# The first x, its halo and the weights of a fused convolution and maxout kernel, loaded and prepared in another way

## The chip, the cores and the metric

The kernel runs on one core of a Trainium2 chip. The metric is the time on the device in microseconds (us); lower is better. Every time below comes from the profiled execution or from the timed runs of this kernel.

## What is computed

Two steps follow one another. The first is a causal convolution of width 7 along the sequence whose weights are made for each position and head by a softmax. The second is a maxout layer: two products with a hidden width of 1024, their elementwise maximum, and a product back to 192.

```python
# x: (8, 4160, 192), weight_gen: (8, 4160, 8 heads, 7 taps)
w = softmax(weight_gen, axis=-1)
x_pad = concatenate([zeros((B, 6, D)), x], axis=1)
y[b, s, h, g] = sum_k w[b, s, h, k] * x_pad[b, s + k, h, g]     # 24 channels a head
# moe_w1, moe_w2: (192, 1024), moe_w_out: (1024, 192)
out = maximum(y @ w1, y @ w2) @ w_out                           # (33280, 192) fp32
```

The kernel uses max(a, b) = a + relu(b - a): `wd` holds w2 - w1, `w10` holds w1 @ w_out, and out = relu(y @ wd) @ w_out + y @ w10.

## The kernel before

**Tiling.** The 33280 positions are cut into 128 partitions of 260 consecutive positions, so 16 partitions make one sequence. Each partition's 260 positions are worked on in 16 batches of 16 positions and a last one of 4. A partition needs the six positions ahead of its first one as well, the halo. For 112 of the 128 partitions the halo is the end of the partition before; for every sixteenth partition, where a sequence begins, it must be zero. `msk` holds 0 or 1 for each partition, and the halo of the first batch is multiplied by it. Later batches copy their halo from the batch before (the second DMA in `load_x`).

**Stages of a batch.** `exp_sum`, `red`, `ln`, `shift` and `weights` make the normalised tap weights `en_t` (ScalarE and VectorE in turn). `mul` is the VectorE product of x and the weights for all seven taps (L177). For the first batches the taps are summed and transposed by TensorE (`sum_transpose`, L243) and copied to `yt` by ScalarE (L250); later, VectorE adds the taps and a DMA transposes. `hid_tile` (L279) computes y @ wd on TensorE, `relu` (L289) evicts it on ScalarE, and `out_first`/`out_second` (L331 with `w10`, L319 with `wo`) make the output in PSUM. `evac` copies it out.

**Order.** The schedule is written out by hand: each engine runs its instructions in the order of the program text, and SyncE and GpSimd issue DMAs in that order too. SyncE's go into a hardware queue, GpSimd's into a software queue. From the fourth group of tiles on, a loop over groups of tiles issues the rest.

**The beginning, where the change lies.** SyncE issues `weight_gen` of batch 0 (L105), the halo of partitions 16 to 127 (L500), the first four positions of x (L507), four loads with the first 512 columns of w1 and w2 (L518; E is rows 0 to 127 and T rows 128 to 191, so `ws0E`, `ws1E`, `ws0T`, `ws1T`), positions 4 to 7, the other 512 columns, and `weight_gen` of batch 1. GpSimd issues the halo of partitions 1 to 15, and makes a partition index (L529) and the identity. All this x arrives as fp32 in `xs`. GpSimd (L540) and ScalarE (L542) multiply one half of the halo each by the mask into the bf16 tile `xb_t`. VectorE casts positions 0 to 3 (L546), and ScalarE positions 4 to 7 (L553). The first `mul` (L177) follows. `keep_warm` runs products of the identity on TensorE (L598) until then. VectorE subtracts w1 from w2 for half of the columns (L557, L561), ScalarE copies pieces of the result to the other partitions (L559, L560, L563); for the second half VectorE does both.

GpSimd waits for the last weight load of the first half with a one-element copy (`gate`, L566) and then issues further x loads, which cast to bf16 on the way, and `wo`. It also casts `w1T` (L573). `w1` in bf16 is transposed (L586), evicted (L648) and multiplied with `wo` on TensorE (L630), and five ScalarE copies (L642) put the result into `w10`.

Of the kernel before, what the change touches and what calls it, by code (L numbers as in the profile page):

```python
# [9 lines left out]
FP32 = mybir.dt.float32  # L10
BF16 = mybir.dt.bfloat16
I32 = mybir.dt.int32
AF = mybir.ActivationFunctionType
ALU = mybir.AluOpType
# [9 lines left out]
def kernel(  # L24
# [85 lines left out]

    def load_x(b, o, n, amid=lambda: None):

        if b not in xb_ts:
            xb_ts[b] = pxb.tile([P, (16 + PAD) * D], BF16, name="xb_t", tag="xb")
        nc.gpsimd.dma_start(  # L115
            out=xb_ts[b][:, (PAD + o) * D:(PAD + o + n) * D],
            in_=bass.AP(tensor=x.tensor, offset=(BATCHES[b][0] + o) * D,
                        ap=[[CPP * D, P], [1, n * D]]),
        )
        amid()  # L120
        if b > 0 and o == 0:
            nc.gpsimd.dma_start(out=xb_ts[b][:, 0:PAD * D],
                                in_=xb_ts[b - 1][:, 16 * D:(16 + PAD) * D])
# [367 lines left out]
    with tc.tile_pool(name="pstage", bufs=1) as pstage:  # L491
        ident_f = pstage.tile([P, P], FP32, name="ident_f")
        xs = pstage.tile([P, (PAD + 8) * D], FP32, name="xs")
        ws = {(kind, wi): pstage.tile([nr, F], FP32, name=f"ws{wi}{kind}")
              for kind, nr in (("E", P), ("T", 64)) for wi in range(2)}

        load_wg(0, nc.sync)
        nc.vector.memset(xs[0:1, 0:PAD * D], 0.0)
        for p0, p1, eng in ((16, P, nc.sync), (1, 16, nc.gpsimd)):
            eng.dma_start(  # L500
                out=xs[p0:p1, 0:PAD * D],
                in_=bass.AP(tensor=x.tensor, offset=(p0 * CPP - PAD) * D,
                            ap=[[CPP * D, p1 - p0], [1, PAD * D]]),
            )

        def load_first(o):
            nc.sync.dma_start(  # L507
                out=xs[:, (PAD + o) * D:(PAD + o + 4) * D],
                in_=bass.AP(tensor=x.tensor, offset=o * D, ap=[[CPP * D, P], [1, 4 * D]]),
            )  # L510

        load_first(0)
        HF = F // 2

# [8 lines left out]

        load_w(0)
        load_first(4)
        load_w(1)
        load_wg(1, nc.sync)

        nc.gpsimd.iota(msk_i, pattern=[[0, 1]], base=0, channel_multiplier=1)  # L529
        make_identity(nc, ident_f)  # L530
        nc.vector.tensor_single_scalar(out=msk_i, in_=msk_i, scalar=RPB - 1, op=ALU.bitwise_and)
        nc.vector.tensor_single_scalar(out=msk_i, in_=msk_i, scalar=1, op=ALU.min)
        nc.vector.tensor_copy(out=msk, in_=msk_i)
        nc.vector.tensor_copy(out=ident, in_=ident_f)  # L534
        for step in (exp_sum, red, ln, shift):
            for i in range(2):
                step(0, i, 2)
        xb_ts[0] = pxb.tile([P, (16 + PAD) * D], BF16, name="xb_t", tag="xb")
        HP = PAD * D // 2
        nc.gpsimd.tensor_scalar(out=xb_ts[0][:, 0:HP], in0=xs[:, 0:HP], scalar1=msk[:, 0:1], scalar2=None,  # L540
                                op0=ALU.mult)
        nc.scalar.activation(out=xb_ts[0][:, HP:2 * HP], in_=xs[:, HP:2 * HP], func=AF.Copy,  # L542
                             scale=msk[:, 0:1])
        for o in (0, 4, 8, 12):
            weights(0, o)
        nc.vector.tensor_copy(out=xb_ts[0][:, PAD * D:(PAD + 4) * D],  # L546
                              in_=xs[:, PAD * D:(PAD + 4) * D])
        mul(0, 0)
# [3 lines left out]
        nc.scalar.copy(out=w1["E"][:, 0:HF], in_=ws["E", 0][:, 0:HF])  # L552
        nc.scalar.copy(out=xb_ts[0][:, (PAD + 4) * D:(PAD + 8) * D], in_=xs[:, (PAD + 4) * D:])  # L553
        def w_diff(h, copy):
# [17 lines left out]
        )  # L572
        load_x(1, 0, 8, lambda: nc.gpsimd.tensor_copy(out=w1["T"], in_=ws["T", 0]))  # L573
        load_wg(2, nc.gpsimd)
# [25 lines left out]

        keep_warm(27)
        w_diff(0, nc.scalar.copy)
# [4 lines left out]

        nc.scalar.copy(out=w1["E"][:, HF:F], in_=ws["E", 0][:, HF:F])
        rd = room(0)
# [15 lines left out]
        def w10_product():  # L625

            pw = ps["o"].tile([P, 1024], FP32, name="pw", tag="op")
            for at, c0, nr in ((0, 0, P), (512, P, 64)):
                for fi in range(FCH):
                    nc.tensor.matmul(  # L630
                        pw[0:nr, at:at + D], lhsT=w1t[:, fi * D + c0:fi * D + c0 + nr],
                        rhs=wo[:, fi * D:(fi + 1) * D],
                        start=(fi == 0), stop=(fi == FCH - 1), skip_group_check=True,
                    )
            return pw

        def w10_copies(pw):

            for k, to, frm, at in ((0, 0, 0, 0), (1, 0, 64, 0), (2, 64, 0, 0), (1, 64, 0, 512),
                                   (2, 0, 0, 512)):  # L640
                nr = P if k == 0 else 64
                nc.scalar.copy(out=w10[to:to + nr, k * D:(k + 1) * D],  # L642
                               in_=pw[frm:frm + nr, at:at + D])

# [149 lines left out]
```

## Time and profile before

| | |
|---|---|
| median of 5 runs | 412.73 us (412.67 to 413.33) |
| profiled execution, own time | 412.73 us |
| its span, as the trace counts it | 410.9 us |
| TensorE busy | 397.8 us, 97% |
| VectorE busy | 376.7 us, 92% |
| ScalarE busy | 358.1 us, 87% |
| GpSimd busy | 81.6 us, 20% |
| granted TensorE clock | 1.00 |

Times in the profile run from the start of the span. A timeline row gives the start, the duration, the engine, the line in the program, the operation with its output and inputs, the shape and the count; in brackets stands how long the engine was idle before it and who ended that wait. Engine names: PE is TensorE, PEld its weight load, DVE VectorE, ACT ScalarE, POOL GpSimd, SP SyncE; a q behind a name means the engine's queue. The profiled execution took as long as the median, and about 1.8 us of it lie outside the span.

### The profile page before, as it was taken

How to read it: one execution, taken by the hardware profiler on the slowest of the kernel's cores; microseconds unless marked ns; L12 is line 12 of the kernel's file. 1: busy time of each engine (PE TensorE's matmuls, PEld its weight loads, DVE VectorE, ACT ScalarE, POOL GpSimd, SP SyncE). 2: the span in 40 equal slices, each digit the busy share in tenths (PEclk: the TensorE clock that was granted, in tenths of full speed). 3: DMA queues.
4: the chain of work that ended last, by engine and by line, in shares of the span. 5: the costliest groups of instructions: out<-in, count | busy, mean ns of one | idle time of the engine just before them, and what ended most of it. 6: DMA issues, size and time to landing. Idle time of an engine off the chain costs nothing.

```text
span 410.9 us, 15917 instructions
## 1 busy us (share of the span) xinstructions
PE 397.8 (97%) x7309; PEld 316.1 (77%) x7309; DVE 376.7 (92%) x219; ACT 358.1 (87%) x426; POOL 81.6 (20%) x104
## 2 busy tenths in 40 slices
PE   7898899999999999999999999999999999999995
PEld 2588899677777777777877778777777777787795
DVE  5999999999999999999999999999999999999100
ACT  6898998989989998899998999998989989888771
POOL 3720101222211212212012222210212222110000
PEclk9999999999999999999999999999999999999999
DMA  8975535765656965784785586478649637643613
GB/s 243 258 179 164 127 92 137 179 153 141 172 120 146 214 171 124 217 171 112 154 240 148 112 238 171 98 214 205 137 95 257 170 53 246 156 90 88 205 58 139
DMA packets 60242, 65.68 MB, mean 160 GB/s; under 512 B 47601, under 2 KB 48497, under 8 KB 60176
## 3 DMA queue, kind: packets, MB, share of 16 engines
q1 hardware_dynamic: 51904, 40.47, 34.1%
q0 software_dynamic: 8128, 24.11, 28.8%
q8 instruction: 57, 0.93, 0.9%
q10 hardware_dynamic: 144, 0.10, 0.1%
q14 instruction: 9, 0.07, 0.1%
HBM read 35.96 MB, written 25.56 MB: 150 GB/s over the span
## 4 chain that ended last, share of the span: by engine, by line
PE 83%; ACT 10%; issue 3%; DMA 2%; DVE 1%; SPq 1%; DVEq 0%; ACTq 0%
PE op_ps L319 38%; PE hd L279 36%; PE op_ps L331 7%; ACT rd_t L289 6%; DMA ws1T<-in_moe_w_dram 2%; ACT en_t L162 1%; PE hdp L279 1%; ACT o_t L375 1%; DVE wd L557 1%; ACT yt L250 0%; ACT e_t L130 0%; SPq L518 0%; ACT w1t L648 0%; DVE wd L561 0%; ACT w L642 0%
## 5 line engine op out<-in xcount | busy, mean ns | idle before, releaser
L289 ACT ACTIVATE rd_t<-hd 128x1024 bf16<-128x1024 f32 (+1 forms) x206 | 234.6, 1189 | 27.5 <-PE hd L279 26.1
L319 PE MATMUL op_ps<-wo,rd_t 64*128 64x192 bf16 x4160 | 210.5, 243 | 0.1
L319 PEld LDWEIGHTS <-rd_t 64*128 64x128 bf16 x4160 | 180.8, 94 | 15.7 <-ACTq L352 0.3
L279 PE MATMUL hd<-yt,wd 64*128 64x512 bf16 (+1 forms) x1584 | 187.3, 360 | 1.1 <-ACT rd_t L289 1.1
L177 DVE TENSOR_TENSOR m_t<-xb_t,en_t 128x10752 bf16<-128x10752 bf16 (+1 forms) x37 | 187.5, 5069 | 0.6 <-POOL xb_t L540 0.6
L279 PEld LDWEIGHTS <-wd 64*128 64x128 bf16 x1776 | 93.9, 94 | 44.8 <-issue 3.8
L219 POOL CAST gate<-yt 128x1 f32<-128x1 bf16 x29 | 41.3, 1425 | 272.4 <-DMA yt<-y_t 272.4
L193 DVE TENSOR_TENSOR m_t<-m_t 128x4608 bf16<-128x4608 bf16 (+1 forms) x33 | 78.1, 2368 | 0.1
L375 ACT COPY o_t<-op_ps 128x384 f32<-128x384 f32 (+1 forms) x99 | 57.2, 590 | 13.2 <-PE op_ps L319 12.9
L331 PE MATMUL op_ps<-w,yt 64*128 64x192 bf16 x780 | 55.5, 243 | 1.8 <-ACT o_t L375 1.4
L331 PEld LDWEIGHTS <-yt 64*128 64x128 bf16 x780 | 38.4, 94 | 18.5 <-issue 3.2
L199 DVE TENSOR_TENSOR m_t<-m_t 128x3072 bf16<-128x3072 bf16 (+1 forms) x29 | 49.9, 1722 | 0.1
L162 ACT ACTIVATE en_t<-wg_t 128x896 bf16<-128x896 f32 (+2 forms) x45 | 35.2, 816 | 0.3 <-DVE m_t L177 0.3
L202 DVE TENSOR_TENSOR y_t<-m_t 128x1536 bf16<-128x1536 bf16 (+1 forms) x29 | 27.3, 940 | 0.5
L365 DVE COPY o_t<-op_ps 128x192 f32<-128x192 f32 x1 | 0.4, 358 | 25.2 <-ACT o_t L365 25.2
L151 DVE TENSOR_TENSOR wg_t<-wg_t,sum_t 128x280 f32<-128x280 f32 (+5 forms) x46 | 22.0, 480 | 0.0
L115 POOL DMA_DIRECT2D xb_t<-in_x_dram x32 | 17.3, 540 | 22.6 <-DVE m_t L177 22.0
L142 DVE TENSOR_REDUCE sum_t<-e_t 128x64 f32<-128x448 f32 (+2 forms) x31 | 19.5, 633 | 2.3 <-ACT e_t L130 2.2
L130 ACT ACTIVATE e_t<-wg_t 128x896 f32<-128x896 f32 (+2 forms) x18 | 16.1, 898 | 2.6 <-DMA wg_t<-in_weight_gen_dram 2.6
L289 ACT ACTIVATE rd_t<-hdp 128x1024 bf16<-128x1024 f32 x16 | 16.1, 1033 | 2.2 <-PE hdp L279 2.1
L279 PE MATMUL hdp<-yt,wd 64*128 64x256 bf16 x192 | 12.9, 269 | 1.9 <-issue 0.7
L598 PE MATMUL warm<-ident 128*128 128x512 bf16 x33 | 10.4, 485 | 3.0 <-DVE ident L534 3.0
(47 smaller groups left out, 79.9 us busy)
## 6 DMA issues: line engine op xcount, KB each, us to landing
out_dram<-o_t SPq DMA_DIRECT2D x28, 768.0 KB, 5.1
xb_t<-in_x_dram POOLq DMA_DIRECT2D x28, 384.0 KB, 4.9
wg_t<-in_weight_gen_dram POOLq DMA_DIRECT2D x14, 448.0 KB, 5.7
xb_t<-xb_t POOLq DMA_DIRECT2D x16, 288.0 KB, 5.2
out_dram<-o_t SPq DMA_DIRECT2D x8, 384.0 KB, 2.6
wg_t<-in_weight_gen_dram SPq DMA_DIRECT2D x2, 448.0 KB, 4.8
xs<-in_x_dram SPq DMA_DIRECT2D x2, 384.0 KB, 6.6
xb_t<-in_x_dram POOLq DMA_DIRECT2D x1, 768.0 KB, 7.6
```

The lines of the kernel that those rows point to most:

```text
L151: nc.vector.tensor_tensor(out=w_t, in0=w_t, in1=_sub(s_ts[b], hs.start, [[1, hs.stop - hs.start], [0, K]]), op=ALU.subtract)
L162: nc.scalar.activation(out=_sub(en_ts[b], (o * WGC + j * N * K) * 2, [[2 * N, K], [2, N], [1, 2]]), in_=_sub(wg_ts[b], (o * H + j * N) * K ...
L177: nc.vector.tensor_tensor(out=m_out, in0=x_in, in1=_sub(en_ts[b], o * WGC * 2, [[2, K * n * H], [0, G // 2], [1, 2]]), op=ALU.mult,)
L193: nc.vector.tensor_tensor(out=taps(0, 1, 3), in0=taps(0, 1, 3), in1=taps(3, 1, 3), op=ALU.add)
L199: nc.vector.tensor_tensor(out=taps(0, 2, 2), in0=taps(0, 2, 2), in1=taps(1, 5, 2), op=ALU.add)
L202: nc.vector.tensor_tensor(out=_sub(y_ts[b], o * D, [[64, 2], [P, 3 * w // 2], [1, 64]]), in0=taps(0, 1, 1), in1=taps(2, 1, 1), op=ALU.add,)
L219: nc.gpsimd.tensor_copy(out=gate, in_=yt[:, 0:1])
L279: nc.tensor.matmul(hid_out(t, f, j), lhsT=wd[half(j), s * F + f * P:s * F + (f + 1) * P], rhs=_sub(yt_ts[u][half(j), :], (s + j) % 3 * P, ...
L289: nc.scalar.activation(out=rd[:, k * 1024:(k + n) * 1024], in_=hd[:, at:at + n * 1024], func=AF.Relu)
L319: return nc.tensor.matmul(op_out(c), lhsT=rd[half(r), k * 1024 + at:k * 1024 + at + P], rhs=wo[half(r), f * D:(f + 1) * D], start=False, s ...
L331: nc.tensor.matmul(op_out(c + j), lhsT=yt_ts[u][half(j), (3 * i + (s + j) % 3) * P:(3 * i + (s + j) % 3 + 1) * P], rhs=w10[half(j), s * D: ...
L375: nc.scalar.copy(out=_sub(o, c % 24 * D, [[D, len(qs)], [h * D, 2], [1, D]]), in_=_sub(tile_, at + (qs[0] - p) * D, [[D, len(qs)], [512, 2 ...
```

## The change

The first x comes through GpSimd's software queue, which casts to bf16 on the way into `xb_t`: halo and positions 0 to 3 together for partitions 16 to 127 and 1 to 15, positions 0 to 3 for partition 0, then positions 4 to 7. These four DMAs stand behind the partition index and the identity in GpSimd's order. The tile `xs` goes. One VectorE operation multiplies the whole halo by the mask, in place and in bf16; the two half operations on GpSimd and ScalarE and the casts of x on VectorE and ScalarE go. A one-element VectorE copy from `weight_gen` into `ws0E` makes SyncE's first weight load, and all loads behind it, wait for `weight_gen` of batch 0. The cast of `w1T` moves from GpSimd to ScalarE, in two halves. There is one more `keep_warm` product (28 for 27). The product for `w10` writes all 128 rows in its second part too, and three ScalarE copies in place of five move it.

```diff
--- before.py
+++ after.py
@@ -108,7 +108,7 @@
                         ap=[[CPP * WGC, P], [1, n * WGC]]),
         )
 
-    def load_x(b, o, n, amid=lambda: None):
+    def load_x(b, o, n):
 
         if b not in xb_ts:
             xb_ts[b] = pxb.tile([P, (16 + PAD) * D], BF16, name="xb_t", tag="xb")
@@ -117,7 +117,6 @@
             in_=bass.AP(tensor=x.tensor, offset=(BATCHES[b][0] + o) * D,
                         ap=[[CPP * D, P], [1, n * D]]),
         )
-        amid()
         if b > 0 and o == 0:
             nc.gpsimd.dma_start(out=xb_ts[b][:, 0:PAD * D],
                                 in_=xb_ts[b - 1][:, 16 * D:(16 + PAD) * D])
@@ -490,26 +489,26 @@
 
     with tc.tile_pool(name="pstage", bufs=1) as pstage:
         ident_f = pstage.tile([P, P], FP32, name="ident_f")
-        xs = pstage.tile([P, (PAD + 8) * D], FP32, name="xs")
         ws = {(kind, wi): pstage.tile([nr, F], FP32, name=f"ws{wi}{kind}")
               for kind, nr in (("E", P), ("T", 64)) for wi in range(2)}
 
         load_wg(0, nc.sync)
-        nc.vector.memset(xs[0:1, 0:PAD * D], 0.0)
-        for p0, p1, eng in ((16, P, nc.sync), (1, 16, nc.gpsimd)):
-            eng.dma_start(
-                out=xs[p0:p1, 0:PAD * D],
-                in_=bass.AP(tensor=x.tensor, offset=(p0 * CPP - PAD) * D,
-                            ap=[[CPP * D, p1 - p0], [1, PAD * D]]),
+        xb_ts[0] = pxb.tile([P, (16 + PAD) * D], BF16, name="xb_t", tag="xb")
+        nc.vector.memset(xb_ts[0][0:1, 0:PAD * D], 0.0)
+        nc.gpsimd.iota(msk_i, pattern=[[0, 1]], base=0, channel_multiplier=1)
+        make_identity(nc, ident_f)
+        for p0, p1, c0 in ((16, P, -PAD), (1, 16, -PAD), (0, 1, 0)):
+            nc.gpsimd.dma_start(
+                out=xb_ts[0][p0:p1, (PAD + c0) * D:(PAD + 4) * D],
+                in_=bass.AP(tensor=x.tensor, offset=(p0 * CPP + c0) * D,
+                            ap=[[CPP * D, p1 - p0], [1, (4 - c0) * D]]),
             )
-
-        def load_first(o):
-            nc.sync.dma_start(
-                out=xs[:, (PAD + o) * D:(PAD + o + 4) * D],
-                in_=bass.AP(tensor=x.tensor, offset=o * D, ap=[[CPP * D, P], [1, 4 * D]]),
-            )
-
-        load_first(0)
+        load_x(0, 4, 4)
+        nc.vector.tensor_single_scalar(out=msk_i, in_=msk_i, scalar=RPB - 1, op=ALU.bitwise_and)
+        nc.vector.tensor_single_scalar(out=msk_i, in_=msk_i, scalar=1, op=ALU.min)
+        nc.vector.tensor_copy(out=msk, in_=msk_i)
+        nc.vector.tensor_copy(out=ident, in_=ident_f)
+        nc.vector.tensor_copy(out=ws["E", 0][:, 0:1], in_=wg_ts[0][:, 0:1])
         HF = F // 2
 
         def load_w(h):
@@ -522,35 +521,21 @@
                     )
 
         load_w(0)
-        load_first(4)
         load_w(1)
         load_wg(1, nc.sync)
-
-        nc.gpsimd.iota(msk_i, pattern=[[0, 1]], base=0, channel_multiplier=1)
-        make_identity(nc, ident_f)
-        nc.vector.tensor_single_scalar(out=msk_i, in_=msk_i, scalar=RPB - 1, op=ALU.bitwise_and)
-        nc.vector.tensor_single_scalar(out=msk_i, in_=msk_i, scalar=1, op=ALU.min)
-        nc.vector.tensor_copy(out=msk, in_=msk_i)
-        nc.vector.tensor_copy(out=ident, in_=ident_f)
         for step in (exp_sum, red, ln, shift):
             for i in range(2):
                 step(0, i, 2)
-        xb_ts[0] = pxb.tile([P, (16 + PAD) * D], BF16, name="xb_t", tag="xb")
-        HP = PAD * D // 2
-        nc.gpsimd.tensor_scalar(out=xb_ts[0][:, 0:HP], in0=xs[:, 0:HP], scalar1=msk[:, 0:1], scalar2=None,
-                                op0=ALU.mult)
-        nc.scalar.activation(out=xb_ts[0][:, HP:2 * HP], in_=xs[:, HP:2 * HP], func=AF.Copy,
-                             scale=msk[:, 0:1])
+        nc.vector.tensor_scalar(out=xb_ts[0][:, 0:PAD * D], in0=xb_ts[0][:, 0:PAD * D], scalar1=msk[:, 0:1],
+                                scalar2=None, op0=ALU.mult)
         for o in (0, 4, 8, 12):
             weights(0, o)
-        nc.vector.tensor_copy(out=xb_ts[0][:, PAD * D:(PAD + 4) * D],
-                              in_=xs[:, PAD * D:(PAD + 4) * D])
         mul(0, 0)
         w1 = {kind: pstage.tile([nr, F], BF16, name="w1" + kind)
               for kind, nr in (("E", P), ("T", 64))}
 
         nc.scalar.copy(out=w1["E"][:, 0:HF], in_=ws["E", 0][:, 0:HF])
-        nc.scalar.copy(out=xb_ts[0][:, (PAD + 4) * D:(PAD + 8) * D], in_=xs[:, (PAD + 4) * D:])
+        nc.scalar.copy(out=w1["T"][:, 0:HF], in_=ws["T", 0][:, 0:HF])
         def w_diff(h, copy):
 
             c0, c1, c2 = (slice(s * F + h * HF, s * F + (h + 1) * HF) for s in range(3))
@@ -570,7 +555,7 @@
             out=wo[:, :].rearrange("p (f d) -> p f d", d=D),
             in_=bass.AP(tensor=moe_w_out.tensor, offset=0, ap=[[D, P], [P * D, FCH], [1, D]]),
         )
-        load_x(1, 0, 8, lambda: nc.gpsimd.tensor_copy(out=w1["T"], in_=ws["T", 0]))
+        load_x(1, 0, 8)
         load_wg(2, nc.gpsimd)
         load_x(1, 8, 8)
         load_wg(3, nc.gpsimd)
@@ -598,14 +583,15 @@
                 nc.tensor.matmul(warm[:, 0:512], lhsT=ident, rhs=_sub(ident, 0, [[0, 4], [1, P]]),
                                  start=True, stop=True, skip_group_check=True)
 
-        keep_warm(27)
+        keep_warm(28)
         w_diff(0, nc.scalar.copy)
         sum_transpose(0)
         keep_warm(6)
         mul(0, 4)
 
 
-        nc.scalar.copy(out=w1["E"][:, HF:F], in_=ws["E", 0][:, HF:F])
+        for kind in ("E", "T"):
+            nc.scalar.copy(out=w1[kind][:, HF:F], in_=ws[kind, 0][:, HF:F])
         rd = room(0)
         hid_tile(0)
         relu(rd, 0, 1)
@@ -625,10 +611,10 @@
         def w10_product():
 
             pw = ps["o"].tile([P, 1024], FP32, name="pw", tag="op")
-            for at, c0, nr in ((0, 0, P), (512, P, 64)):
+            for at, c0 in ((0, 0), (512, 64)):
                 for fi in range(FCH):
                     nc.tensor.matmul(
-                        pw[0:nr, at:at + D], lhsT=w1t[:, fi * D + c0:fi * D + c0 + nr],
+                        pw[:, at:at + D], lhsT=w1t[:, fi * D + c0:fi * D + c0 + P],
                         rhs=wo[:, fi * D:(fi + 1) * D],
                         start=(fi == 0), stop=(fi == FCH - 1), skip_group_check=True,
                     )
@@ -636,11 +622,9 @@
 
         def w10_copies(pw):
 
-            for k, to, frm, at in ((0, 0, 0, 0), (1, 0, 64, 0), (2, 64, 0, 0), (1, 64, 0, 512),
-                                   (2, 0, 0, 512)):
-                nr = P if k == 0 else 64
-                nc.scalar.copy(out=w10[to:to + nr, k * D:(k + 1) * D],
-                               in_=pw[frm:frm + nr, at:at + D])
+            nc.scalar.copy(out=_sub(w10, 0, [[D, 2], [1, D]]), in_=_sub(pw, 0, [[512, 2], [1, D]]))
+            for to, frm, at in ((64, 0, 0), (0, 64, 512)):
+                nc.scalar.copy(out=w10[to:to + 64, 2 * D:3 * D], in_=pw[frm:frm + 64, at:at + D])
 
 
         hidden(2)
```

## The prediction

> **What bounds the kernel now.** I read the shares by engine and the chain of waits first, then the busy table by stretch, then each engine's timeline over the first 30 us, where every edited line lies.
>
> ```profile
> PE 397.8 (97%) x7309; PEld 316.1 (77%) x7309; DVE 376.7 (92%) x219; ACT 358.1 (87%) x426; POOL 81.6 (20%) x104
> PE 83%; ACT 10%; issue 3%; DMA 2%; DVE 1%; SPq 1%; DVEq 0%; ACTq 0%
> ```
> ```profile
> 0.00:12.00 12.00, 8.89 (x27) 3.29 (x27) 7.56 (x12) 7.01 (x16) 4.70 (x11) 1.00 0.88 264
> 12.00:20.00 8.00, 6.66 (x215) 5.26 (x217) 7.85 (x9) 6.95 (x11) 6.03 (x8) 1.00 1.22 227
> 20.00:30.00 10.00, 9.20 (x279) 7.78 (x275) 9.97 (x6) 9.89 (x19) 2.71 (x6) 1.00 0.74 187
> 30.00:50.00 20.00, 17.81 (x508) 16.67 (x504) 20.00 (x11) 18.37 (x29) 1.06 (x2) 1.00 0.56 147
> 50.00:80.00 30.00, 29.64 (x590) 27.28 (x588) 29.97 (x18) 27.45 (x35) 3.79 (x6) 1.00 0.54 133
> ```
> The columns are the stretch, its length, busy time of PE, PEld, DVE, ACT, POOL, then clock, DMA share and GB/s. From 50 us TensorE idles hardly at all (0.36 us in 30, and 320 us from 80 to 400 hold 319.18 us of PE). Its work there is untouched, so the end moves by as much as the start of that stretch. Before 50 us TensorE waits: all its work before 12 us is `warm`, and 12 to 50 us hold 4.3 us of idle. There the order is set by VectorE (full from 12 us) and ScalarE (9.89 of 10 us from 20 to 30).
>
> VectorE and ScalarE, a few rows of their timelines (start, duration):
> ```profile
> 7.73 0.69 DVE L546 CAST xb_t<-xs 128x768 bf16<-128x768 f32 x1 [0.32 <-DMA xs<-in_x_dram]
> 9.04 2.96 DVE L177 TENSOR_TENSOR m_t<-xb_t,en_t 128x5376 bf16<-128x5376 bf16 x1 [0.61 <-POOL xb_t L540]
> 11.91 0.68 DVE L557 TENSOR_TENSOR wd<-ws1E,ws0E 128x512 bf16<-128x512 f32 x1
> 15.98 1.53 DVE L557 TENSOR_TENSOR wd<-ws1E,ws0E 128x512 bf16<-128x512 f32 x1
> ```
> ```profile
> 12.63 0.62 ACT L559 COPY wd<-wd 64x512 bf16<-64x512 bf16 x1 [0.33 <-DVE wd L557]
> 14.54 0.80 ACT L250 CAST yt<-yps 128x768 bf16<-128x768 f32 x1
> 15.23 0.62 ACT L608 CAST w1E<-ws0E 128x512 bf16<-128x512 f32 x1
> 16.26 1.02 ACT L289 ACTIVATE rd_t<-hdp 128x1024 bf16<-128x1024 f32 x1 [0.40 <-PE hdp L279]
> 19.99 1.94 ACT L289 ACTIVATE rd_t<-hdp 128x1024 bf16<-128x1024 f32 x2 [0.26 <-PE hdp L279]
> 27.59 1.55 ACT L642 CAST w<-pw 128x192 bf16<-128x192 f32 x5
> ```
> ```profile
> 1.27 0.67 POOL L500 DMA_DIRECT2D xs<-in_x_dram  x1 [0.84 <-POOLq L778]
> 7.06 1.95 POOL L540 TENSOR_SCALAR xb_t<-xs,msk 128x576 bf16<-128x576 f32 x1 [4.35 <-DVE wg_t L151]
> 14.55 2.42 POOL L573 CAST w1T<-ws0T 64x1024 bf16<-64x1024 f32 x1
> ```
> The first product (L177 at 9.04) waits last for GpSimd's half of the halo mask, 7.06 to 9.01. All else hangs on that product: two wd differences, three ScalarE copies, yt, first hidden tile, first relu at 16.26. (The chain of waits itself enters this stage through `DMA ws1T` to 10.66; I don't follow it, because L557 begins at 11.91 when the product ends, not when the weights land.)
>
> **What the Trainium skill says.** *SBUF — State Buffer*, "SBUF: two separate sides": a VectorE operation with two SBUF inputs and a GpSimd operation that reads SBUF exclude one another. The trace agrees: L557 costs 0.68 us alone and 1.53 us while POOL's L573 runs (14.55 to 16.97). *DMA: Bandwidth & Descriptors*, "Anatomy of one DMA — SWDGE (gpsimd) path": a GpSimd DMA costs about 2.0 us plus bytes/436 GB/s. The trace has 4.4 us for the 384 KB issued at 11.98 and 5.6 us for 67.5 KB issued at 1.27, so more when the start is crowded. The same page, "Queues, rings and completion order": an engine takes turns between the rings that have work, packet by packet. I use that for how x and the weights share.
>
> **The change, part by part.** S is the start of the first product, now 9.04.
>
> 1. *x and halo.* SP's two early x issues and the 4..8 one go; POOL issues four cast DMAs instead, now after iota and identity. Those took 2.03 to 2.70; moved up to 1.27 they end near 1.95. The first issue is then near 1.95, the others about 0.65 later each (row L500): 2.6, 3.2, 3.9. Bytes read: 112 rows x 7,680 B = 860 KB, 15 rows = 115 KB, 3 KB, then 393 KB. Price of the first by the skill: 2.0 + 2.0 = 4.0, landing at 5.9; the 15 rows run behind, 0.3 us more. By the trace's nearest crowded row the fixed part is up to 5.6 instead of 2.0: landing near 9.5. The likely value lies near the low end, since only the 448 KB of weight_gen (used from 4.59) is ahead of it: I take 7.0 for landing with the halo rows, and 5.9 and 9.5 as ends.
> 2. *Mask.* POOL 1.95 (L540) and ACT 0.78 (L542) go, with the cast L546 0.69; VectorE gets one 128x1152 bf16 multiply. Nearest row: the bf16 copy 64x512 at 0.29. 1152/512 of it is 0.65, with a fixed part less; I take 0.5 (0.35 to 0.7). It follows the second `shift`, which ends at 7.41, and can run at 7.45: S = 7.45 + 0.5 + semaphores, 8.0 if x is there, 8.3 as I take it. The other input, en, is no limit: ScalarE without L542 starts it near 6.9 instead of 7.59. **S moves by -0.7** (ends -1.0 and, with x at 9.5, +1.0).
> 3. *Weights released by weight_gen.* VectorE's one-element copy into ws0E waits for wg0 (about 4.55), costs about 0.1 us and delays nothing: the next VectorE work waits for `exp` until 5.2. SP's eight weight issues and wg1 queue behind it: first at 4.8 instead of 2.11, then one each 0.5 us, ws1T of half 0 at 6.3 instead of 3.74. The 768 KB of half 0 took from 6.7 to near 10 us at 300 to 400 GB/s; now about 5.9 to 9.5 with 393 KB of x between, landing near 10 (10.66 before). L557 needs it at S+2.9 = 11.2. Cost 0, with 1 us of cover; POOL's gate, L566, and the loads behind it move with ws1T, and the product that reads them (20.2) has 1.8 us. Half 1 and wg1 were landed by 15; their bytes follow directly, and I expect them by 13.5.
> 4. *w1T on ScalarE.* Half 0's copy (64x512, 0.6 us like L552) replaces L553 (0.83, which waited 0.92 for x) before the wd copies: free. Half 1's, 0.62, comes between L608 and the first relu. There 0.40 us is idle, so relu comes about **+0.3** later after yt (0.92 now, 1.25 then).
> 5. *POOL's w1T cast gone.* Half 1's L557 drops from 1.53 to 0.68: VectorE gains another 0.85, so its stream runs 1.5 us early. ScalarE's idle of 0.26 before 19.99, a wait for tiles that need the half-1 wd, closes: **-0.25**.
> 6. *w10.* Five copies, 1.55 us, become one of 128x384 (the 128x384 eviction L375 is 0.5) and two of 64x192 (0.31 each): 1.1. ScalarE is full there and TensorE's first output product (29.19) waits for it: **-0.45**. The product's second half has 128 instead of 64 columns of weights; the 192 moving columns, 247 against 249 ns, cost the same: 0.
> 7. *keep_warm 28.* 27 take 8.89 us, so 28 take 9.2. They wait for `ident`, which moves from 2.97 to about 2.3; they end near 11.5, where the product ends at 11.2. The 0.3 us is hidden: yt needs ScalarE, which is in the wd copies until S+5.6 = 13.9, while the transposes end at 12.9.
>
> Sum on the ScalarE path: -0.7 + 0.3 - 0.25 - 0.45 = **-1.1 us**. VectorE, 1.5 early, stays ahead of it. Own time of the profiled execution is 412.73 us (span 410.9 and 1.8 around it), equal to the median of the five runs, so 411.6.
>
> **Rivals.**
> - *Mostly absorbed.* Behind 29 us lie waits of TensorE that are nobody's work: 0.72 "issue" at 34.34, and 0.91 for an eviction at 42.83. If they grow by half of what was gained, -0.5: 412.2. For: the 4.3 us of idle come from changing partners. Against: ScalarE, 18.37 of 20 us, and VectorE, 20 of 20, both start earlier.
> - *The cast transfer lands late: slower.* One mechanism at one place: the software queue's first packets start late, 3.5 us after issue as for the 67.5 KB of L500 (issued 1.27, first packet 4.8 in the packet records), that is at 5.5, when the weights are also running, and x's 2.5 us of packets share the engines and land at 9.5 to 10.5. VectorE then masks, S = 10.1 to 11. From the sum, the break-even is S = 9.04 + 0.4 = 9.4, x landed near 8.9. At S = 10.4 the change costs +1.0: 413.7. For: that row. Against: its packets had two hardware transfers in front, now one; GpSimd issues later in the run (27.66, 44.73) have first packets after 1.25 us.
> - *The weights become late.* Same result as no gain if ws1T lands at 12 or later; 2 us beyond my figure, and then 412.7.
>
> **How the numbers follow.** About 0.2%, 0.83 us, is what a measurement of this kernel can tell from no change. Main case, S 8.0 to 8.7, -1.4 to -0.7: 0.60. Absorbed or weights late, -0.7 to 0: 0.18. Late x, +0.2 to +1.9: 0.22. Nearly nine tenths of the main case lie beyond -0.83, and a quarter of the late case stays within 0.83: faster 0.53, same 0.30, slower 0.17. Likeliest 411.6; range 410.9 (S 8.0, mask 0.35, and one TensorE wait gone) to 413.4 (S about 10.1), while the main case alone spans 411.2 to 412.1.
>
> **What would show it.** L177's first start: 8.3 right, above 9.4 wrong. The DMA wait before the mask small; ws1T landed before 11; half-1 L557 near 0.7; the row before the first relu without idle and its start near 15.9; L642's successors 1.1 us together; first output product near 28.1; the PE rows from 50 us on shifted by one amount. A mask or product that waits for `xb_t<-in_x_dram` beyond 8.9, or TensorE idling for over 0.5 us after `warm`, makes the prediction wrong.

## The result and the profile after

The changed kernel is slower: 414.65 us (413.17 to 417.21 in 43 runs) against 413.04 us for the kernel before in the same runs, a ratio of 1.0036 with an interval of 1.0029 to 1.0043. The forecast was 411.6 (410.9 to 413.4). The profiled execution of the changed kernel took 413.67 us, its span 411.9; that is 0.94 us over the profiled execution of before, so about 0.7 of the median's 1.6 us is not in this trace. I come back to it with the clock, behind the last experiment.

The page first: shares by engine, the chain of waits, one group, one DMA queue.

```profile
PE 396.4 (96%) x7310; PEld 316.0 (77%) x7310; DVE 375.4 (91%) x220; ACT 357.3 (87%) x424; POOL 79.0 (19%) x105
...
q8 instruction: 57, 0.93, 0.9%
...
PE 81%; ACT 13%; DMA 3%; issue 2%; SPq 0%; DVE 0%; ACTq 0%; DVEq 0%
...
L318 PE MATMUL op_ps<-wo,rd_t 64*128 64x192 bf16 x4160 | 210.8, 243 | 1.1 <-issue 1.0
```

Every engine has less work and the kernel takes longer. The last row is a place to start: of the 1.1 us TensorE idles ahead of its largest group, 1.0 is one stall labelled "issue". The q8 row will matter below: 57 packets of 16,384 bytes, the queue that brings TensorE's own instructions.

The busy table by stretch (length, busy of PE, PEld, DVE, ACT, POOL, then clock, DMA share, GB/s):

```profile
12.00:20.00 8.00, 6.54 (x217) 5.25 (x219) 7.59 (x10) 7.40 (x11) 3.02 (x6) 1.00 1.16 219
20.00:30.00 10.00, 8.49 (x259) 7.14 (x257) 9.97 (x6) 9.95 (x18) 3.39 (x7) 1.00 0.95 230
30.00:50.00 20.00, 17.69 (x492) 16.72 (x486) 20.00 (x11) 16.95 (x27) 1.06 (x2) 1.00 0.55 142
```

ScalarE still had 9.95 of 10 us from 20 to 30, but between 30 and 50 it fell from 18.37 to 16.95 us: there it is waiting for TensorE. VectorE's timeline (start, duration, engine, line, operation, in brackets the idle time before it and who ended it):

```profile
8.86 0.52 DVE L529 TENSOR_SCALAR xb_t<-xb_t,msk 128x1152 bf16<-128x1152 bf16 x1 [1.88 <-DMA xb_t<-in_x_dram]
9.47 2.96 DVE L176 TENSOR_TENSOR m_t<-xb_t,en_t 128x5376 bf16<-128x5376 bf16 x1
12.35 0.68 DVE L542 TENSOR_TENSOR wd<-ws1E,ws0E 128x512 bf16<-128x512 f32 x1
13.30 0.68 DVE L546 TENSOR_TENSOR wd<-ws1T,ws0T 64x512 bf16<-64x512 f32 x1 [0.27 <-DMA ws1T<-in_moe_w_dram]
...
16.78 0.68 DVE L542 TENSOR_TENSOR wd<-ws1E,ws0E 128x512 bf16<-128x512 f32 x1
```

The first product starts at 9.47, not 8.3, and waits for the transfer of x. After it the weights are late too. Rows of ScalarE and GpSimd show how much:

```profile
10.86 0.62 ACT L537 CAST w1E<-ws0E 128x512 bf16<-128x512 f32 x1 [1.91 <-DMA ws0E<-in_moe_w_dram]
12.53 0.62 ACT L538 CAST w1T<-ws0T 64x512 bf16<-64x512 f32 x1 [1.05 <-DMA ws0T<-in_moe_w_dram]
...
16.81 1.02 ACT L288 ACTIVATE rd_t<-hdp 128x1024 bf16<-128x1024 f32 x1
```
```profile
13.27 0.17 POOL L551 COPY gate<-ws1T 64x1 f32<-64x1 f32 x1 [9.50 <-DMA ws1T<-in_moe_w_dram]
13.38 1.06 POOL L115 DMA_DIRECT2D xb_t<-in_x_dram  x2
```

In the kernel before, the gate and the loads behind it came earlier:

```profile
10.72 1.32 POOL L566 COPY gate<-ws1T 64x1 f32<-64x1 f32 x1 [1.71 <-DMA ws1T<-in_moe_w_dram]
11.98 1.17 POOL L115 DMA_DIRECT2D xb_t<-in_x_dram  x2
```

The first relu is 0.55 us late (16.81 for 16.26). But the lag does not stay. Counting the relu instructions from 1 in both traces, it is +0.16 at the third, −0.04 at the seventh (26.63 us) and −0.27 at the eighth (29.37), because steps 5 and 6 give the time back. Then it jumps to +0.78 at the ninth and +1.16 at the tenth, and stays there to about 300 us (the span ends +0.95). So the loss arises between 29 and 37 us. TensorE's timeline there:

```profile
27.28 1.13 PE L242 MATMUL yps<-ident,m_t 64*128 64x64 bf16 x65
29.68 0.46 PE L242 MATMUL yps<-ident,m_t 64*128 64x64 bf16 x19 [1.27 <-issue]
...
34.30 0.82 PE L318 MATMUL op_ps<-wo,rd_t 64*128 64x192 bf16 x15
36.15 0.25 PE L318 MATMUL op_ps<-wo,rd_t 64*128 64x192 bf16 x1 [1.04 <-issue]
```

A run of 84 equal transposes breaks after 65 for 1.27 us, and a run of 16 products after 15 for 1.04. No operand is missing there: the same tiles feed both sides of each break. The kernel before runs its 84 transposes in one piece, and has one such stall:

```profile
27.40 1.40 PE L243 MATMUL yps<-ident,m_t 64*128 64x64 bf16 x84
...
35.06 0.83 PE L279 MATMUL hdp<-yt,wd 64*128 64x256 bf16 x12 [0.72 <-issue]
```

**What the stalls are.** Count TensorE's instructions in program order, a weight load and its product as two. The 84 transposes that break begin at instruction 829; 65 pairs later is 959. The 16 products that break begin at 1185; 15 pairs later is 1215. The stall of before is at 1215 too, and every "issue" stall of a TensorE product over 0.15 us, in every trace of this study, stands at 447, 703, 959, 1215, 1471 or 1983: on one grid with steps of 256, wherever that falls in the program. 16,384 bytes over 256 instructions is 64 bytes each, and TensorE's 14,620 records make 57 such blocks, as many as q8 has packets. The Trainium skill, *Runtime: NRT & Kernel Launch*, section "Instruction fetch mechanics", describes it: the sequencer refills its instruction memory in 16 KiB blocks of 256 instructions through a DMA queue of its own, and the cost of crossing a boundary is "mostly hidden". In these two traces it is hidden from 50 us on, where no wait of TensorE is longer than 0.36 us and none is "issue", and it is not hidden in the crowded start. Times of the packets in that queue's records, and the stalls:

| kernel | block needed at 959: packet, stall | block needed at 1215: packet, stall |
|---|---|---|
| before | 25.93–26.84, none | 32.64–33.99, 0.72 |
| after | 27.20–28.15, 1.27 | 33.86–34.84, 1.04 |

TensorE resumes 1.1 to 1.5 us after the packet ends, and in none of the fourteen traces of this study does it enter any block sooner than 1.07 us after that block's packet. That ties the stalls to the packets. The order of the records suggests that a block is asked for when TensorE enters the block ahead of it: behind the crowded start, from the ninth block on, the packet begins a median 0.5 us after that crossing in both traces. Both kernels cross instruction 703 near 24.1 us, and the packet for 959 starts 1.8 us later in before and 3.1 in after; they cross 959 near 28.4 and 29.7, and the packet for 1215 starts 4.3 and 4.2 us later. The DMA engines are meanwhile busy with GpSimd's loads: the one 16-position x load of batch 2 has 128 packets of 586 ns, which is 4.7 us on each of 16 engines if they are spread evenly. The changed kernel's loads behind `gate` are issued at 13.38 instead of 11.98, and the `weight_gen` and x packets that follow end at 28.85 instead of 27.33. That this traffic is what holds the block back is up to here an inference; the experiments test it.

### The profile page after: what moved, and what is told of

It reads as the page before. It is cut to its first block, busy times and chain, and to the rows that moved or that the text cites. A ratio compares the mean times of both kernels' runs of the same rounds, so it can differ in the third digit from the quotient of the medians.

```text
span 411.9 us, 15911 instructions
## 1 busy us (share of the span) xinstructions
PE 396.4 (96%) x7310; PEld 316.0 (77%) x7310; DVE 375.4 (91%) x220; ACT 357.3 (87%) x424; POOL 79.0 (19%) x105
## 4 chain that ended last, share of the span: by engine, by line
PE 81%; ACT 13%; DMA 3%; issue 2%; SPq 0%; DVE 0%; ACTq 0%; DVEq 0%
PE op_ps L318 38%; PE hd L278 36%; PE op_ps L330 7%; ACT rd_t L288 7%; DMA ws0T<-in_moe_w_dram 2%; ACT en_t L161 1%; ACT yt L249 1%; DMA wg_t<-in_weight_gen_dram 1%; ACT o_t L374 1%; ACT e_t L129 1%; PE hdp L278 0%; ACT w1t L632 0%; SPq L517 0%; ACT sum_t L145 0%; ACT wd L544 0%
## 5 line engine op out<-in xcount | busy, mean ns | idle before, releaser
L218 POOL CAST gate<-yt 128x1 f32<-128x1 bf16 x29 | 42.8, 1477 | 272.5 <-DMA yt<-y_t 272.5
L278 PE MATMUL hdp<-yt,wd 64*128 64x256 bf16 x192 | 13.2, 269 | 1.0 <-ACT yt L249 0.6
L242 PE MATMUL yps<-ident,m_t 64*128 64x64 bf16 x528 | 9.4, 190 | 4.4 <-DVE m_t L176 3.1
```

The lines of the kernel that those rows point to most:

```text
L218: nc.gpsimd.tensor_copy(out=gate, in_=yt[:, 0:1])
L278: nc.tensor.matmul(hid_out(t, f, j), lhsT=wd[half(j), s * F + f * P:s * F + (f + 1) * P], rhs=_sub(yt_ts[u][half(j), :], (s + j) % 3 * P, ...
```

## The experiments

**One part alone: w10 and w1T (e2).** The kernel before, with steps 4 to 6 of the change and nothing of x, halo and release.

```diff
-        load_x(1, 0, 8, lambda: nc.gpsimd.tensor_copy(out=w1["T"], in_=ws["T", 0]))
+        load_x(1, 0, 8)
+        nc.scalar.copy(out=w1["T"][:, 0:HF], in_=ws["T", 0][:, 0:HF])
...
+        for kind in ("E", "T"):
+            nc.scalar.copy(out=w1[kind][:, HF:F], in_=ws[kind, 0][:, HF:F])
...   (w10_product and w10_copies as in the change)
```


> The kernel before with only the parts away from x: w1T cast by ScalarE in two halves (the first one ahead of the copy of x 4..7), no GpSimd cast, w10 in three copies. By the prediction's steps 4 to 6 (+0.3, -0.25, -0.45) the first output product comes 0.4 us earlier and the time is 0.4 below the kernel before, 412.6 for 413.0; half 1's L557 takes 0.7 instead of 1.53. Rival: what counts from 28 us on is when TensorE's instruction blocks of 16,384 bytes arrive, not ScalarE; then the product starts earlier but the end moves by 0 or by the length of another stall of 0.7 to 1.3 us.

Measured: 413.29 us, ratio 1.0008 (0.9994 to 1.0021), no difference: the forecast of −0.4 missed, and its rival described what happened. TensorE in the profiled execution (412.48 us):

```profile
26.45 1.14 PE L243 MATMUL yps<-ident,m_t 64*128 64x64 bf16 x66
28.00 0.44 PE L243 MATMUL yps<-ident,m_t 64*128 64x64 bf16 x18 [0.42 <-issue]
28.27 0.42 PE L331 MATMUL op_ps<-w,yt 64*128 64x192 bf16 x6
...
35.03 0.83 PE L279 MATMUL hdp<-yt,wd 64*128 64x256 bf16 x12 [1.60 <-issue]
```

The first output product starts 0.92 us earlier (28.27 for 29.19), and the relu rows are 0.6 to 0.9 early from 22 to 34 us. Then TensorE stands at instruction 1215 for 1.60 us in place of 0.72 and resumes at 35.03, where before resumed at 35.06. The gain is taken whole by a wait that doesn't move with the engines, because the block arrives by the DMA queues' time (packet end 33.6 here, 33.99 before).

**The release left out (e1).**

```diff
-        nc.vector.tensor_copy(out=ws["E", 0][:, 0:1], in_=wg_ts[0][:, 0:1])
```


> The kernel after without the one-element copy that makes the weight loads wait for weight_gen. If x's software queue is what holds the weights up once it runs (weights issued at 4.35 had their first packet at 8.16 us), the weights, issued from 1.2 us on, get ahead of x: the last half-0 weight lands near 9 instead of 13.2, but x shares the engines from its first packet and the mask starts at 10 to 11 instead of 8.86; the time is 414.5 to 415.5. Rival: the release is the whole loss; x lands at 8.9 all the same, the weights no longer hold VectorE up, and the time falls to 413 or below.

Measured: 415.13 us, ratio 1.0052 (1.0032 to 1.0072), as forecast. The weights land near 10.0 instead of 13.2, and x at 9.95 instead of 8.8: the first product starts at 10.55 and the first relu 2.17 us late. Issue stalls of 0.57, 2.05 and 0.52 stand at 447, 703 and 1215. Part of the late relu is the clock's: the first 84 transposes took 2.42 us for 1.40, at half the granted clock (more on this below). So x and weights compete for the same time; the release moved the delay from x to the weights, and was not the error. GpSimd's loads behind the gate left at 10.45 here, earlier than in before (11.98), and the stalls came all the same: what counts is which traffic a block's request meets, not only how late the loads are.

**More warming (e3).**

```diff
-        keep_warm(28)
+        keep_warm(40)
```


> The kernel after with 40 keep_warm products instead of 28. If the 2.9 us of TensorE idle between the last warm product and the first transpose let the clock drop in part of the executions (clocks of 0.990 to 0.998 in most of its runs), the granted clock is 0.998 or more throughout, the scatter of 413.2 to 417.2 narrows and the median falls by 0.5 to 1. Rival: the idle is harmless; the median stays at 414.6 with the same scatter.

Measured: 416.27 us, ratio 1.0079 (1.0066 to 1.0092). Neither the forecast nor its rival expected a longer time. The profiled execution kept the full clock, with 0.26 us of idle ahead of the first transposes, so the clock does not make it slow. The 24 more instructions ahead move every later one, and the stalls move in the program but not in number: what broke after 65 transposes now breaks elsewhere.

```profile
25.74 0.68 PE L242 MATMUL yps<-ident,m_t 64*128 64x64 bf16 x35 [1.07 <-issue]
...
31.09 0.64 PE L242 MATMUL yps<-ident,m_t 64*128 64x64 bf16 x31 [1.04 <-issue]
```

These are instructions 703 and 959; further stalls, 1.63 and 1.00, are at 1215 and 1983. The break follows the count, not the operation. The weights landed late in this run too (13.9 for the change's 13.2), so what the twelve products alone cost isn't shown.

**Halo apart, x on all partitions (e4; f4 without the release).**

```diff
-        for p0, p1, c0 in ((16, P, -PAD), (1, 16, -PAD), (0, 1, 0)):
+        for p0, p1 in ((16, P), (1, 16)):
             nc.gpsimd.dma_start(
-                out=xb_ts[0][p0:p1, (PAD + c0) * D:(PAD + 4) * D],
+                out=xb_ts[0][p0:p1, 0:PAD * D],
...
+        load_x(0, 0, 4)
         load_x(0, 4, 4)
```


> The kernel after with the halo (112 rows and 15 rows of 1152) and positions 0 to 3 (one transfer of 128 rows of 768) as separate cast transfers; same bytes. If the transfer of 112 rows of 1920 is slow because about 8 of the 16 engines carry its second half (packets until 8.44 us at 13 per 0.5 us), the 128-row transfer uses all 16, the mask starts near 7.5 instead of 8.86, the first product near 8.1 to 8.5 instead of 9.47, and the time falls by about 1 us. Rival: the software queue is as slow in any shape; the mask starts at 8.5 to 9.2 and the time stays within 0.4.

> The kernel with halo and positions 0 to 3 as separate cast transfers, and the weights not released by weight_gen. There x had landed at 7.0 and the first product began at 7.98, but the weights came at 13.1 and VectorE waited 1.5 us for them. Without the release the weights land near 9.5 and x near 8.5 to 9; the first product begins at 8.5 to 9.5 and no wd difference waits. If instruction blocks decide, the time need not follow: 413 to 414.5; if the start decides, 412.3 to 413.

Measured: e4 413.78 us, ratio 1.0018 (1.0003 to 1.0034); f4 414.99, ratio 1.0044 (1.0032 to 1.0056). VectorE in e4:

```profile
7.98 2.96 DVE L176 TENSOR_TENSOR m_t<-xb_t,en_t 128x5376 bf16<-128x5376 bf16 x1 [0.42 <-ACT en_t L161]
11.94 0.69 DVE L543 TENSOR_TENSOR wd<-ws1E,ws0E 128x512 bf16<-128x512 f32 x1 [1.00 <-DMA ws1E<-in_moe_w_dram]
13.11 0.68 DVE L547 TENSOR_TENSOR wd<-ws1T,ws0T 64x512 bf16<-64x512 f32 x1 [0.48 <-DMA ws1T<-in_moe_w_dram]
```

With the halo and the first positions apart, x is there by 7.1 and the product waits for the tap weights alone: 7.98, the 8.0 that step 2 gave for "if x is there". In the change, the packets of the joint transfers ran from 3.34 to 8.44: some 15 were in flight at a time from 5 to 6 us and 8 or 9 from 6.5 to 8, when those of positions 4 to 7 ran beside them (13 to 17 in all). So the engines were not half idle, as the expectation had it. From 3.5 to 5 us the change had 6 to 12 packets in flight and e4 9 to 17. Which property of the transfers makes that difference isn't shown: e4 changes their size and number along with the partitions, and its halo still goes over 112 of them. The 1.5 us gained go to the weights: VectorE waits 1.00 and 0.48, ScalarE 1.45 and 1.24, and the first relu is 0.43 late again. The median is nevertheless 0.9 below the change's, as forecast. The profiled execution, at 414.75 at the upper end of e4's runs, has stalls of 0.63, 1.54 and 1.58 at 447, 959 and 1215, so it doesn't show where that gain arises. f4 missed its forecast. Without the release the 4-position part itself came late, the first product started at 10.30, and relu was 3.08 late, with half the granted clock from 11.8 to 18.6 us as a part of it. No order of these loads that I tried brings both x and the weights by the time of before.

**The gate alone (g2): is the loss the blocks?** e2, with the one-element gate reading a column of the second half of ws1T, so that GpSimd's loads wait for the later weight load. Nothing else is changed.

```diff
-        nc.gpsimd.tensor_copy(out=gate[0:64, :], in_=ws["T", 1][:, 0:1])
+        nc.gpsimd.tensor_copy(out=gate[0:64, :], in_=ws["T", 1][:, HF:HF + 1])
```


> The kernel of w10 and w1T alone (x as before), with the gate on the second half of ws1T, which lands near 14 us: the loads behind it come 2 to 2.5 us later, all else stays. If late GpSimd loads cost through the instruction blocks, the block behind instruction 703 starts after 27 instead of 25.7, TensorE stalls at instruction 959 for 1 to 2 us (0.42 without the delay), and the time rises by 0.7 to 1.5 over that kernel's 413.3. Rival: the start of the first product made the loss in the kernel after; here it is unchanged at 9.04 and the time stays within 0.3.

Measured: 414.49 us, ratio 1.0031 (1.0022 to 1.0041), against e2's 413.29: +1.2 us, as forecast (+1.0 by the two ratios). GpSimd's and TensorE's rows:

```profile
14.05 1.83 POOL L567 COPY gate<-ws1T 64x1 f32<-64x1 f32 x1 [5.28 <-DMA ws1T<-in_moe_w_dram]
15.83 1.17 POOL L115 DMA_DIRECT2D xb_t<-in_x_dram  x2
```
```profile
26.61 1.14 PE L243 MATMUL yps<-ident,m_t 64*128 64x64 bf16 x66
30.11 0.44 PE L243 MATMUL yps<-ident,m_t 64*128 64x64 bf16 x18 [2.36 <-issue]
```

The loads go at 15.83 (11.98 in before and e2). The relu rows stay 0.2 to 1.0 early up to 29 us, so nothing is late there; then instruction 959 costs 2.36 us (packet 27.8–28.8), and the first output product is 1.19 us late (30.38 for 29.19). ScalarE waits once for a late load itself, 0.47 us for `weight_gen` until 30.1, and right behind that 3.31 for TensorE, so that wait is covered. The next relu is 2.70 late, later ones 1.8 to 1.9. Not all of the 2.70 is the stall's: behind it the granted clock was half from 31.2 to 34.6 us, and 48 products took 3.63 us where before they took 2.44.

```profile
31.85 3.63 PE L319 MATMUL op_ps<-wo,rd_t 64*128 64x192 bf16 x48
```
```profile
31.00:35.00 4.00, 3.89 (x60) 3.38 (x56) 4.00 (x3) 1.33 (x4) 1.07 (x2) 0.57 0.97 227
```

The time doesn't rest on that stretch: 3.4 us at half clock take 0.004 off a run's mean clock, 19 of the 22 runs have a mean of 0.997 or more, and their median is 414.46. So later loads behind the gate are enough for a loss of this size, with x untouched. The delay here is 3.85 us, though, and the change's is 1.40; that 1.40 alone would do it is not shown by this run.

**The batch-2 load in four parts (f1 on before, f2 on e2, f3 on after).** The question is whether smaller loads on GpSimd let the block for 1215 in between.

```diff
-        load_x(2, 0, 16)
+        for o in (0, 4, 8, 12):
+            load_x(2, o, 4)
```
f3 also splits `load_x(1, 8, 8)` in two.

> The kernel before with x of batch 2 loaded in four transfers of 4 positions instead of one of 16, back to back in the same place; same bytes. TensorE's only stall without a partner (0.72 us at instruction 1215) ends 1.07 us after a 16,384-byte instruction block that started at 32.64, 3.7 us after the 16-position transfer had begun to occupy the engines (8 packets of 586 ns on each). If the block waits for one whole transfer's packets on its engine, it now waits for 1.1 us at most, starts near 30, the stall goes and the time falls by about 0.7, to 412.3. Rival: the block waits for all that GpSimd has queued, or for something else; the stall and the time stay.

> The kernel of w10 and w1T alone with the same four transfers. There the first output product came 0.9 us earlier than before but the stall at instruction 1215 grew from 0.72 to 1.60 us and ended at the same 35.0. If instruction blocks are what ate the gain, both stalls go and the time is 1.3 to 1.7 below the kernel before, 411.3 to 411.7. Rival: ScalarE takes over; within 0.4 of f1's time.

> The kernel after with x of batch 2 in four transfers of 4 positions and the second half of batch 1 in two of 4. Its stalls at instructions 959 (1.27 us) and 1215 (1.04) follow blocks that started at 27.20 and 33.86. If the size of the software transfers ahead of them is the cause, most of the 2.3 us goes, the time falls by 1.5 to 2.2 to 412.5 to 413.2 and the scatter shrinks. Rival: the late first product and late weights are the loss, not the blocks; the time stays above 414.

Measured: f1 412.87 us, ratio 0.9998 (0.9990 to 1.0006); f2 412.06, 0.9985 (0.9974 to 0.9996); f3 413.87, 1.0026 (1.0012 to 1.0040). The block for 1215 comes at 30.4–31.5 in f1 and 31.0–32.0 in f2 (32.7–33.6 in e2), and the stall there is gone in both. f2 keeps e2's gain this time, less 1.11 us at the next block, and so stays short of its forecast:

```profile
28.01 0.44 PE L243 MATMUL yps<-ident,m_t 64*128 64x64 bf16 x18 [0.60 <-issue]
...
39.60 0.59 PE L319 MATMUL op_ps<-wo,rd_t 64*128 64x192 bf16 x10 [1.11 <-issue]
```

f1 is a miss in its time. Its rows are 0.68 us early from 40 us on, as the missing stall demands, and in the profiled execution they lose 0.9 again near 277 us, where a hidden product waits 0.71 for the DMA that writes `yt`. Whether that happens in its other runs I can't tell; the time says that something does. f3 is 0.8 faster than the change, half of the least that was forecast: its stall at 1215 shrank to 0.21, and the one at 959 grew to 1.82 (packet 28.6–29.5). Why it grew isn't shown.

**Loads spread by progress (g3 on e2).** Two of the four parts go when they did; the other two and `weight_gen` of batch 4 wait for `yt` of groups 4 and 5.

```diff
-        load_x(2, 0, 16)
-        load_wg(4, nc.gpsimd)
+        load_x(2, 0, 4)
+        load_x(2, 4, 4)
...
+    def later(u, *loads):
+        nc.gpsimd.tensor_copy(out=gate, in_=yt_ts[u][:, 0:1])
+        for load in loads:
+            load()
...   (after group 4: load_x(2, 8, 4); after group 5: load_x(2, 12, 4), load_wg(4))
```


> The kernel of w10 and w1T alone with x of batch 2 in four transfers of 4 positions, the third and fourth issued only after yt of units 4 and 5, and weight_gen of batch 4 behind them. With four transfers back to back TensorE still stalled 0.60 at instruction 959 and 1.11 at 1471. If what is queued decides, the stall at 1471 shrinks below 0.5 and the time is 411.3 to 411.9 (412.06 there). Rival: the blocks are late for another reason; 412.0 to 412.5.

Measured: 412.08 us, ratio 0.9974 (0.9962 to 0.9985): with f2 the fastest of the study and faster than both kernels, 2.6 us below the change. Stalls of 0.59 and 0.78 remain at 959 and 1215, none at 1471. The stall went as forecast; the time is no better than f2's, where the rival had it.

**The change with its gate mended (g1), and with g3's loads as well (g4).** The gate follows the first weight load instead of the fourth.

```diff
-        nc.gpsimd.tensor_copy(out=gate[0:64, :], in_=ws["T", 1][:, 0:1])
+        nc.gpsimd.tensor_copy(out=gate, in_=ws["E", 0][:, HF - 1:HF])
```


> The kernel after with one edit: GpSimd's gate reads the last half-0 column of ws0E instead of ws1T, so the x, wo and weight_gen loads behind it are issued near 11 us instead of 13.3 (before: 12.0). If the lateness of these loads is what delays TensorE's instruction block behind instruction 703 (it started at 27.2 instead of 25.9), that block starts by 26, the stall of 1.27 at instruction 959 goes and the time falls by 1 to 1.3. Rival: the loads collide with the weights instead, the first relu moves from 16.8 to 17.5 and the time stays or grows.

> The kernel after with both edits: the gate on ws0E and batch 2's x spread as above. If instruction blocks were the whole loss, its two stalls (1.27 and 1.04) go and it reaches 412.0 to 412.6, as far behind the kernel with x as before as its first relu is later (0.5). Rival: the late weights keep it above 413.5.

Measured: g1 414.42 us, ratio 1.0033 (1.0024 to 1.0042); g4 413.53, ratio 1.0007 (0.9995 to 1.0018), no difference from before. g1 fails, as its rival said: the gate's copy took 1.40 us, the loads left at 12.53, 0.85 earlier only, and the two T weights landed later still (13.35 and 14.05). Whether the loads took their DMA time isn't shown, since in e3, with the old gate, they landed at 13.2 and 13.9. Stalls of 0.71 and 1.03 remained. g4 has no issue stall at all and brings back 1.1 of the 1.6 us; it too ends where its rival was, just above 413.5. What keeps it above e2 and g3 is for the most part in its first rows on TensorE and its clock:

```profile
12.62 2.42 PE L242 MATMUL yps<-ident,m_t 64*128 64x64 bf16 x84 [2.98 <-DVE m_t L176]
14.97 2.74 PE L583 MATMUL warm<-ident 128*128 128x512 bf16 x6
```
```profile
12.00:30.00 18.00, 16.96 (x446) 13.52 (x448) 16.04 (x14) 15.46 (x23) 6.16 (x11) 0.82 0.99 215
```

The 28 `warm` products ended at 9.6, TensorE idled 2.98 us, and the clock granted from 12 to 30 us was 0.82: the 84 transposes took 2.42 us, where in before and after they took 1.40. The first relu came 2.67 us late; by 40 us 0.85 of that was left, and another 0.6 was lost at 279 us, where a hidden product waits 0.44 for the DMA that writes `yt`, the same wait as in f1.

**The clock.** The clock records behind the 0.82 show half clock from 11.7 to 18.5 us. f4 has the same, and e1, f3 and g1 have half clock for 3.4 us between 13.0 and 17.4. In all five TensorE had idled for 1.75 to 3.62 us between `warm` and the first transposes. The profiled execution of the changed kernel idled 2.92 there and kept the full clock, but its other runs often didn't: 27 of its 44 (the profiled one included) have a mean clock of 0.996 or less, against 1 of the 71 runs of before in the last round. The other 17 have a median of 414.35. So the clock takes about 0.3 us of the median's 1.6, and the rest is there without it.

Runs of like clock can also be compared with each other. Of g4's 22 runs, 17 are at 0.996 or less (median 413.64) and five are above (412.69). So at full clock, mending the gate and spreading the loads take the changed kernel from 414.35 to 412.69, no slower than before (413.04); g3's 17 runs of this kind stand at 412.07, which leaves some 0.6 us for late x and weights once the blocks are out of the way. Five runs are few, but that is close to the 0.5 that was expected.

What stays open is why the changed kernel's runs at full clock lie 0.7 above its profiled execution. The waits for `yt` near 278 us, which f1 and g4 show and the traces of before and after don't, are one candidate; stalls that vary from run to run are another. I have one profile of each kernel.

## Why the prediction was wrong, point by point

**Step 1 failed: x landed at 8.8, not 7.0.** It was inside the ends that I gave (5.9 and 9.5), but the likely value came from the bytes ahead of it alone. The bytes did not set it: e4 moved as many by 7.1, in other transfers. S came to 9.47, at the late rival's break-even of 9.4, and the first relu was late by 0.55. That rival had the direction. Its mechanism, first packets only at 5.5, is not what happened (3.34), and it priced the loss at this place, where the lag was gone by 27 us.

**Step 2 held**: the mask took 0.52 (forecast 0.5). Its 8.3 for S had 0.3 too much by its own figures, since x at 7.0 would have been there before the mask could start at 7.45; e4, with x by 7.1, measured 7.98.

**Step 3 failed.** ws1T landed at 13.2, not 10. The first weight transfer was issued at 4.35, a little before the forecast 4.8, and its first packet ran at 8.16, when those of the first x transfers were running out (8.44). I had expected the two to share by turns. In e1, where the weights' packets ran first (from 3.31), both did run side by side from 6.5 to 9.5 us; the first packet of a weight load that is issued behind x is what I had wrong. Costed "0, with 1 us of cover", step 3 cost ScalarE 1.91 and 1.05 us of waiting and VectorE 0.27, and, worse, moved the loads behind GpSimd's gate by 1.4 us. That is the rival of late weights (ws1T at 12 or later), which was priced at no gain and no loss. I named only the product at 20.2 as a reader of these loads and held 1.8 us against it. Their other victim, TensorE's instruction blocks, I did not consider.

**Steps 4 to 6 were right or too small.** In e2 the half-1 L557 took 0.68, as forecast; the +0.3 before the first relu was +0.02; the first output product came 0.92 earlier where the sum of −0.25, −0.45 and 0.3 gives 0.4. None of it reached the end, for the reason below.

**Step 7 was wrong, and harmless only in the changed kernel's trace.** 28 products took 7.52 us, not 9.2, because more of them ran at the faster spacing (0.43 us each lasted 2.5 us, in before 5.9). That spacing differs from execution to execution: e2's 27 products, started as in before, took 7.49 against 8.89, and 28 took up to 8.7 (f3). A single measured 8.89 was no price for the next run. That left 2.92 us of idle ahead of the first transposes, which I had put at 0.3 of overlap, and which the prediction had named as a sign of being wrong. In that trace the transposes still took 1.40; over the runs the clock takes about 0.3 us, as shown above.

**The step that decides is the reading of "issue".** The prediction took the 0.72 us at 34.34 as a wait that is "nobody's work" and gave the absorbing rival −0.5 us and, together with the rival of late weights, a part of 0.18. It is the wait for a transfer with its own queue, its own time of request and its own traffic ahead of it. So "the end moves by as much as the start of that stretch" was right in this trace (+1.16 at 40 us, +1.25 at the last relu), but what sets that start is not only ScalarE and VectorE: the arrival of two instruction blocks does. Taking the parts in order: up to 27 us x and weights cost 0.54 (after −0.04, e2 −0.58). Behind that TensorE stalls for 1.27 and 1.04 us, where before has 0.72 alone, and the lag goes from −0.27 to +1.16. g2 shows that moving the gate alone can bring such a stall, and g4 that with both stalls gone the loss is gone too in its five runs at full clock.

## What to carry to other kernels

Where a run of equal instructions breaks with "issue", count the instructions: if breaks are 256 apart, the engine waits for its own program, and the cure is in the DMA queues, not in the operands. Smaller or later loads helped here in f2, g3 and g4; in f1 they removed the stall and left the time as it was. Before a gain ahead of such a stall is counted, ask whether the block's arrival moves with it; if not, the gain is lost whole, as in e2. A load that is released later delays not only its readers but can also delay, through the loads behind it in its queue, the engine's own program (g2).

## What of the hardware was unexpected

- By these records an instruction block comes only about one block ahead of its use, 256 instructions or some 4 to 5 us here: 1.8 us (before) or 4.4 us (g2, which crosses 703 near 23.4) between the crossing and the packet decides between no stall and 2.36 us.
- A cast transfer of halo and four positions over 112 partitions (and 15 more) needed 5.1 us of packets (3.34 to 8.44); with halo and positions apart, the same bytes were there by 7.1.
- A hardware-queue transfer issued at 4.35 had its first packet at 8.16, behind most of the software queue's packets, though its own queue had been empty since about 4.
- An idle of 1.75 to 3.62 us between `warm` and the first transposes went with half the granted clock for 3.4 or 6.8 us in five profiles (e1, f3, f4, g1, g4), and with the full clock in another (after, 2.92). In g2 half clock for 3.4 us followed 1.1 us after a stall of 2.36.
- A one-element copy on GpSimd took from 0.17 us (after) to 1.83 (g2); as a gate it delays the loads behind it by as much.
